# Second layer of a two-layer MLP: seven products in a row, then twelve sets, in place of four alternating blocks

## The chip, the cores and the metric

The kernel runs on one core of one Trainium2 chip. The metric is the time of one execution on the device in microseconds (us), the median of repeated runs. The core has TensorE (matrix products, PE in the profile, its weight loads PEld), VectorE (DVE), ScalarE (ACT), GpSimd (POOL) and SyncE (SP), which here issues every DMA.

## The reference

A linear attention, and two MLPs on its 4608 rows of 512 numbers:

```python
kv = np.einsum('bhsd,bhse->bhde', k_s, v)          # k_s, q_s: softmaxes of k and q
x = np.einsum('bhsd,bhde->bhse', q_s, kv)          # as 4608 rows of 512
h = np.maximum(x @ w_in1, 0.0);  x = (h * h) @ w_out1          # 512 -> 2048 -> 512
h = x @ w_in2;  out = (h * (1.0 / (1.0 + np.exp(-h)))) @ w_out2 # 512 -> 2048 -> 512
```

The weights come in as 64-bit floats. The change concerns the last line alone, the second layer.

## The kernel before, in words

Every operand of a large product is split into a high and a low part that TensorE takes (fp32r), and a product is three matmuls: high x high, high x low, low x high. `split` (L116) makes the parts: a cast on ScalarE (L117) gives the high one, a subtract on VectorE (L118) the low one.

The second layer takes 768 tokens at a time (`TS`), in six steps. In each step it goes through the 2048 hidden units in eight pairs of 128-blocks (`turns`, forward in one step and backward in the next). For a pair, `strassen` (L606) computes h = x @ w_in2 for two hidden blocks and two halves of 384 tokens with seven products in place of eight. Their names are A11, S1, S2, S4, S3, A12, A22, in the order in which they are run. A product (`product`, L597) is six matmuls of 128x384 at L602: two chunks of the inner dimension, three matmuls each. The weights wah and wal are kept per pair, two pairs at a time (`wa`, a `Cache`); in the first step they are made from w_in2, later they are loaded back. The operands x[0] to x[6] are made once per step from the first layer's result: `load_second` loads it (xr), `x_second` makes four differences (xt), and `X.split` splits all seven.

The products use two PSUM tiles, a and c, in turn: A11 on a, S1 on c, S2 on a, S4 on c, S3 on a, A12 on a fresh c, A22 on a. After each product ScalarE copies the tile to h, or VectorE adds it to h: copies at L613 (A11), L616 (S1), L620 (S2) and L636 (A22), adds at L623 (S4), L627 (S3) and L631 (A12). S2, S4, S3 and A22 accumulate onto what a or c holds, so the tile must have been copied before. `silu` (L870) makes g from a finished h: sigmoid (ScalarE, L872), multiply (VectorE, L873) and split into a g of high and low part. It runs twice per pair, for the first hidden block after A12 and for the second after A22.

The second product, y = g @ w_out2, is `y_mm` (L852). It is a generator of twelve sets per pair: for each of the two hidden blocks e and each of six groups of 128 tokens, `mm3` (L187 to L190) adds three matmuls of 128x512 to one of six PSUM banks Y. These hold the sums over all eight pairs; in the last pair of a step each bank is copied to a row tile o (L864, ScalarE and VectorE in turn), which SyncE writes out (L867). Together with a and c they fill all eight banks.

The sets of a pair are not run where they are created. `before` holds the generator of the previous pair, and `fill(n)` runs n sets of it. In `strassen`, `fill(sets)` stands after the second, the fourth and the sixth product and `fill(99)`, the rest, after the seventh; in the second layer `sets` is 3. `hook(n)` is called ahead of the product n and at the end (n = 7); in the second layer it loads, differences and splits the x of the next step at chosen pairs m. The order of the instructions on each engine is then made by a scheduler from the written order and the dependencies; it moves instructions ahead of others that must wait. Within an engine the order is fixed after that.

Of the kernel before, what the change touches and what calls it, by code (L numbers as in the profile page):

```python
# [10 lines left out]
F32 = mybir.dt.float32  # L11
F32R = mybir.dt.float32r
# [9 lines left out]
P = 128  # L22
TB = 512
# [8 lines left out]
def kernel(  # L32
# [15 lines left out]
    NT, DM = out.shape  # L48
# [10 lines left out]
    TS = 768  # L59
    TH = TS // 2  # L60
    assert SC == 4 and SM == TB and B * SL == TB and NB == B + 1 and SL <= P

    NP = NF // 2
# [5 lines left out]
    gpool = ctx.enter_context(tc.tile_pool(name="g", bufs=2))  # L69
# [11 lines left out]
    def take(shape, dt, name):  # L81

        at = idle.pop(0)
        t = spool.tile(shape, dt, tag=f"s{at}", name=name)
        slot_of[id(t)] = (at, t)
        return t
# [29 lines left out]
    def split(hi, lo, src):  # L116
        nc.scalar.copy(hi, src)  # L117
        nc.vector.tensor_sub(lo, src, f32(hi))  # L118
# [343 lines left out]
    def fill(n):  # L462
        for _ in range(n):
            next(before, None)
# [65 lines left out]
    wa = Cache(2, uses, make_wa, load_wa)  # L530
# [60 lines left out]
    def x_second(raw):  # L591
        t = [take([P, 2, NK // 2, TH], F32, "xt") for _ in range(2)]
        u = (slice(0, TH), slice(TH, TS))
        return X(TH, [raw[h][:, :, v] for v in u for h in range(2)],
                 [t[n // 2][:, n % 2] for n in range(4)], raw + t, 1)

    def product(ps, w, q, x, first):  # L597
        for c in range(2):
            k = slice(c * P, (c + 1) * P)
            wh, wl, xh, xl = w[0][:, q, k], w[1][:, q, k], x[:, 0, c], x[:, 1, c]  # L600
            for n, (l, r) in enumerate(((wh, xh), (wh, xl), (wl, xh))):
                nc.tensor.matmul(  # L602
                    ps, l, r, start=first and c == 0 and n == 0, stop=c == 1 and n == 2, skip_group_check=True
                )

    def strassen(w, x, th, h, g_of, hook, sets):  # L606

        new = lambda tag: ps_q.tile([P, TB], F32, tag=tag, name=tag)[:, 0:th]
        one, two = slice(0, th), slice(th, 2 * th)
        hook(0)  # L610
        a, c = new("a"), new("c")
        product(a, w, A11, x[0], True)
        nc.scalar.copy(h[:, 0, one], a)  # L613
        hook(1)
        product(c, w, S1, x[1], True)
        nc.scalar.copy(h[:, 1, two], c)  # L616
        fill(sets)
        hook(2)
        product(a, w, S2, x[2], False)
        nc.scalar.copy(h[:, 0, two], a)  # L620
        hook(3)
        product(c, w, S4, x[3], False)
        nc.vector.tensor_add(h[:, 0, two], c, h[:, 0, two])  # L623
        fill(sets)
        hook(4)
        product(a, w, S3, x[4], False)
        nc.vector.tensor_add(h[:, 1, two], a, h[:, 1, two])  # L627
        hook(5)
        c = new("c")
        product(c, w, A12, x[5], True)  # L630
        nc.vector.tensor_add(h[:, 0, one], c, h[:, 0, one])  # L631
        g = [g_of(h[:, 0])]
        fill(sets)
        hook(6)
        product(a, w, A22, x[6], False)
        nc.scalar.copy(h[:, 1, one], a)  # L636
        g.append(g_of(h[:, 1]))
        fill(99)
        hook(7)
        return g  # L640


    def relu2(h, src):
        nc.scalar.activation(h, src, AF.Relu)  # L644
        nc.scalar.activation(h, h, AF.Square)
        g = gpool.tile([P, 2, TB], F32R, tag="g", name="g")
        split(g[:, 0], g[:, 1], h)
        return g
# [143 lines left out]
    t = 0  # L792
    for j in range(1, NB):
        x, xs = xs, None
        for m, i in enumerate(turns[j - 1]):
            def hook(n):
                if (j, m, n) == (1, 0, 3):
                    wa.want(0)
                if n in (1, 6):
                    next(attend, None)  # L800
                    if j == 1 and (m, n) in ((1, 6), (3, 6)):
                        next(attend, None)
                if j < NB - 1:
                    if m == 4 and n == 0 and j == NB - 2:
                        XR[j + 1] = take([P, NK, TB], F32, "xr")
                        nc.sync.dma_start(out=XR[j + 1], in_=xld.rearrange("k p t -> p k t"))
                    if m == NP - 1:
                        if n == 0:
                            state["x"] = x_first(j + 1)
                            state["x"].split(2)  # L810
                        elif n == 4:
                            x.done(4)
                            state["x"].split(2)
                        elif n == 7:
                            x.done(NQ)
                            state["x"].split(3)
                else:
                    if m == 4 and n == 0:
                        state["raw"] = load_second(0)
                    elif m == 5 and n == 0:  # L820
                        state["x"] = x_second(state["raw"])
                        state["x"].split(2)
                    elif m == 6 and n == 0:
                        state["x"].split(1)
                    elif m == 7 and n == 0:
                        state["x"].split(1)
                    elif m == 7 and n == 4:
                        x.done(4)
                        state["x"].split(2)
                    elif m == 7 and n == 7:  # L830
                        x.done(NQ)
                        state["x"].split(1)

            state = {} if m == 0 else state
            h = hpool.tile([P, 2, TB], F32, tag="h", name="h")
            g = strassen(wa.tiles[0, i], x.x, TB // 2, h, lambda v: relu2(v, v), hook, 2)
            before = out_pair(j, m, i, g)
            t += 1
            wa.want(t)

            if j >= 2 and m < 6:
                next(ahead, None)
        xs = state["x"]
# [4 lines left out]
    lpool = ctx.enter_context(tc.tile_pool(name="l", bufs=2, reuse_waits="tile"))  # L848
# [3 lines left out]
    def y_mm(s, k, g, w):  # L852

        for e in range(2):
            first, last = k == 0 and e == 0, k == NP - 1 and e == 1
            for c in range(TS // P):
                if first:
                    pool, tag = (ps_o, f"o{c}") if c < NK else (ps_a, "pa")
                    Y[c] = pool.tile([P, DM], F32, tag=tag, name=f"y{c}")
                n = slice(c * P, (c + 1) * P)  # L860
                mm3(Y[c], g[e][:, 0, n], g[e][:, 1, n], w[:, 0, e], w[:, 1, e], first, last)
                if last:
                    o = lpool.tile([P, DM], F32, tag="y", name="o", bufs=4)
                    (nc.vector.tensor_copy if c % 2 else nc.scalar.copy)(o, Y[c])  # L864
                    at = s * TS + c * P
                    for r, rows in out_rows(order[at // TB], at % TB // P):
                        nc.sync.dma_start(out=rows, in_=o[r])  # L867
                yield

    def silu(h):  # L870
        z = lpool.tile([P, TS], F32, tag="z", name="z")
        nc.scalar.activation(z, h, AF.Sigmoid)  # L872
        nc.vector.tensor_mul(z, z, h)  # L873
        g = gpool.tile([P, 2, TS], F32R, tag="g", name="g")
        split(g[:, 0], g[:, 1], z)
        return g

    t1 = t
    for s in range(STEPS):
        x, state = xs, {}  # L880
        for m, i in enumerate(turns[NB - 1 + s]):
            def hook(n):
                if s + 1 == STEPS:
                    return
                if m == 1 and n == 0:
                    state["raw"] = load_second(s + 1)
                elif m == 4 and n == 0:
                    state["x"] = x_second(state["raw"])
                elif m == NP - 1 and n == 0:
                    state["x"].split(1)  # L890
                elif m == NP - 1 and n == 4:
                    x.done(4)
                    state["x"].split(3)
                elif m == NP - 1 and n == 7:
                    x.done(NQ)
                    state["x"].split(3)

            h = lpool.tile([P, 2, TS], F32, tag="h", name="h")
            g = strassen(wa.tiles[1, i], x.x, TH, h, silu, hook, 3)
            wb.want(t - t1)  # L900
            before = y_mm(s, m, g, wb.tiles[i,][0])
            t += 1
            wa.want(t)
        xs = state.get("x")
# [31 lines left out]
```

## Time and profile before

| | us |
|---|---|
| median of three runs | 1660.09 |
| the three runs | 1659.59, 1660.09, 1670.22 |
| the profiled execution | 1662.81 |
| its span on the core | 1661.0 |
| TensorE busy in the span | 1610.4 (97%) |
| VectorE, ScalarE busy | 996.2 (60%), 855.8 (52%) |
| TensorE's granted clock over the span | 0.999 |

A profile is one execution. Its timeline gives the start and the duration of each instruction, and in brackets how long the engine was idle before it and what released it. Matmuls are pipelined: the duration of one (0.33 to 0.40 us here) is longer than the distance to the next, so the distance between starts is what counts. The waits list, for a pair of instructions, who waited for whom: microseconds in total, how often, and the longest.

### The profile page before, as it was taken

Reading aid. Unit: us, or ns where it says so; the run is one execution under the profiler, and the core shown is the slowest. Engines: PE = TensorE matmul, PEld = TensorE weight load, DVE = VectorE, ACT = ScalarE, POOL = GpSimd, SP = SyncE. Lnnn points to the kernel's source line nnn. Section 1 sums busy time; section 2 is a strip of 40 time slices with the busy share of each in tenths; the row PEclk is TensorE's granted clock in tenths of the full one; section 3 lists DMA queues with packets and bytes.
Section 4 is the critical chain, followed back from the end, with each engine's and each line's share of the span. In section 5 each row is a group of like instructions: output and inputs, shape, how many; then the busy total and the mean of one; then the engine's idle time right before and its main releaser. Section 6 shows DMA issues by size and latency. Waiting matters only on the chain.

```text
span 1661.0 us, 24854 instructions
## 1 busy us (share of the span) xinstructions
PE 1610.4 (97%) x9624; PEld 1396.8 (84%) x9624; DVE 996.2 (60%) x1695; ACT 855.8 (52%) x1505; POOL 54.4 (3%) x150
## 2 busy tenths in 40 slices
PE   4999999999999999999999999999999999999999
PEld 3566888888888888889998889898988989999897
DVE  7999896886868687642436675345344344444333
ACT  4876675666666565654546554334334334334332
POOL 2000000000001000000000000000000000000000
PEclk9999999999999999999999999999999999999999
DMA  7776767678685776745346864543543543544621
GB/s 207 258 226 192 234 208 255 200 218 240 183 259 156 231 206 221 227 168 199 137 171 244 335 248 161 187 184 123 189 174 128 193 165 134 196 156 148 221 96 39
DMA packets 193510, 320.40 MB, mean 193 GB/s; under 512 B 113264, under 2 KB 142960, under 8 KB 188528
## 3 DMA queue, kind: packets, MB, share of 16 engines
q1 hardware_dynamic: 193392, 318.81, 57.6%
q8 instruction: 76, 1.25, 0.3%
q14 instruction: 42, 0.34, 0.1%
HBM read 248.51 MB, written 70.25 MB: 192 GB/s over the span
## 4 chain that ended last, share of the span: by engine, by line
PE 75%; DVE 10%; DMA 6%; ACT 5%; issue 2%; POOL 1%; SPq 0%; POOLq 0%; DVEq 0%; ACTq 0%
PE a L602 19%; PE c L602 14%; PE y L189 8%; PE y L190 8%; PE y L188 8%; PE op L189 5%; PE op L188 5%; PE op L190 5%; DMA raw<-in_moe_w_in_dram 3%; PE hp L655 2%; DMA raw<-in_moe_w_out_dram 2%; DVE g L118 1%; ACT raw L142 1%; DVE m L275 1%; DVE u L150 1%
## 5 line engine op out<-in xcount | busy, mean ns | idle before, releaser
L602 PE MATMUL a<-x,wah 128*128 128x256 f32 (+1 forms) x1792 | 397.7, 309 | 10.7 <-ACT h L636 6.4
L602 PEld LDWEIGHTS a<-x,wah 128*128 128x128 f32 x1792 | 313.4, 189 | 55.9 <-ACT h L636 11.7
L602 PE MATMUL c<-x,wah 128*128 128x256 f32 (+1 forms) x1344 | 293.4, 305 | 0.2 <-DVE h L623 0.2
L602 PE MATMUL a<-x,wal 128*128 128x256 f32 (+1 forms) x896 | 275.4, 307 | 0.0
L189 PE MATMUL op<-g,w 128*128 128x512 f32 x576 | 229.3, 398 | 3.1 <-DVE g L118 3.1
L188 PE MATMUL op<-g,w 128*128 128x512 f32 x576 | 229.2, 402 | 3.0 <-ACT g L117 3.0
L190 PE MATMUL y<-wb,g 128*128 128x512 f32 x576 | 227.8, 396 | 0.0
L189 PE MATMUL y<-wb,g 128*128 128x512 f32 x576 | 227.4, 395 | 0.0
L602 PEld LDWEIGHTS c<-x,wah 128*128 128x128 f32 x1344 | 225.0, 190 | 1.7 <-DVE h L623 0.6
L190 PE MATMUL op<-g,w 128*128 128x512 f32 x576 | 225.5, 391 | 0.0
L188 PE MATMUL y<-wb,g 128*128 128x512 f32 x576 | 223.2, 389 | 0.4 <-ACT wb L117 0.4
L602 PE MATMUL c<-x,wal 128*128 128x256 f32 (+1 forms) x672 | 204.8, 305 | 0.0
L872 ACT ACTIVATE z<-h 128x768 f32<-128x768 f32 x96 | 81.3, 847 | 226.9 <-DVE h L631 225.7
L602 PEld LDWEIGHTS a<-x,wal 128*128 128x128 f32 x896 | 168.9, 189 | 0.2
L623 DVE TENSOR_TENSOR h<-c,h 128x256 f32<-128x256 f32 (+1 forms) x112 | 53.7, 480 | 190.7 <-PE c L602 189.2
L644 ACT ACTIVATE h<-h 128x512 f32<-128x512 f32 x128 | 80.8, 632 | 105.1 <-DVE h L631 103.7
L118 DVE TENSOR_TENSOR g<-h,g 128x512 fp32r<-128x512 f32 x128 | 88.0, 688 | 77.7 <-ACT g L117 77.4
L118 DVE TENSOR_TENSOR g<-z,g 128x768 fp32r<-128x768 f32 x96 | 91.9, 957 | 67.3 <-ACT g L117 66.9
L627 DVE TENSOR_TENSOR h<-a,h 128x256 f32<-128x256 f32 (+1 forms) x112 | 53.5, 477 | 127.9 <-PE a L602 127.9
L620 ACT COPY h<-a 128x256 f32<-128x256 f32 (+1 forms) x112 | 47.1, 420 | 159.2 <-PE a L602 159.2
L190 PEld LDWEIGHTS op<-g,w 128*128 128x128 f32 x576 | 108.9, 189 | 23.7
L602 PEld LDWEIGHTS c<-x,wal 128*128 128x128 f32 x672 | 127.6, 190 | 0.0
(150 smaller groups left out, 2323.3 us busy)
## 6 DMA issues: line engine op xcount, KB each, us to landing
wah<-wad SPq DMA_DIRECT2D x72, 896.0 KB, 6.5
wal<-wad SPq DMA_DIRECT2D x72, 896.0 KB, 6.0
wb<-wbd SPq DMA_DIRECT2D x30, 1024.0 KB, 4.9
raw<-in_moe_w_in_dram SPq DMA_DIRECT2D x32, 512.0 KB, 5.3
raw<-in_moe_w_out_dram SPq DMA_DIRECT2D x32, 512.0 KB, 5.3
wad<-wah SPq DMA_DIRECT2D x16, 896.0 KB, 4.1
wad<-wal SPq DMA_DIRECT2D x16, 896.0 KB, 5.0
x1d<-o SPq DMA_DIRECT2D x18, 512.0 KB, 5.2
```

What stands on the lines that cost most here:

```text
L118: nc.vector.tensor_sub(lo, src, f32(hi))
L142: first = nc.scalar.activation(f32(lo32), lo32, AF.Copy, scale=2.0 ** -51, bias=2.0)
L188: nc.tensor.matmul(ps, lh, rh, start=first, stop=False)
L189: nc.tensor.matmul(ps, lh, rl, start=False, stop=False)
L190: nc.tensor.matmul(ps, ll, rh, start=False, stop=last)
L602: nc.tensor.matmul(ps, l, r, start=first and c == 0 and n == 0, stop=c == 1 and n == 2, skip_group_check=True)
L620: nc.scalar.copy(h[:, 0, two], a)
L623: nc.vector.tensor_add(h[:, 0, two], c, h[:, 0, two])
L627: nc.vector.tensor_add(h[:, 1, two], a, h[:, 1, two])
L644: nc.scalar.activation(h, src, AF.Relu)
L655: nc.tensor.matmul(hp, f32(w[:, s]), XR[0][:, c], start=c == 0, stop=c == NK - 1)
L872: nc.scalar.activation(z, h, AF.Sigmoid)
```

## The change

In the second layer the three numbers of sets that `strassen` runs between the products become (0, 0, 0): all seven products of a pair run in a row, and `fill(99)` then runs all twelve sets of the previous pair. The first layer keeps two sets in each place. Three things go with it. Every third g comes from a buffer of its own in `lpool`, so that three buffers take turns in place of two. The row tiles o have three buffers in place of four. And the hooks that prepare the next step's x are moved to later products: the differences from the start of the fifth pair to the last product of the fourth, the first split from the start of the last pair to the last product of the one before, and the next three from the fifth product of the last pair to its last. One empty line is added, so that the lines of `strassen` have numbers one higher.

```diff
         nc.scalar.copy(h[:, 1, two], c)
-        fill(sets)
+        fill(sets[0])
...
         nc.vector.tensor_add(h[:, 0, two], c, h[:, 0, two])
-        fill(sets)
+        fill(sets[1])
...
         g = [g_of(h[:, 0])]
-        fill(sets)
+        fill(sets[2])
...
-                    o = lpool.tile([P, DM], F32, tag="y", name="o", bufs=4)
+                    o = lpool.tile([P, DM], F32, tag="y", name="o", bufs=3)
...
-        g = gpool.tile([P, 2, TS], F32R, tag="g", name="g")
+        made.append(len(made) % 3)
+        g = (lpool.tile([P, 2, TS], F32R, tag="g", name="g", bufs=1) if made[-1] == 2 else
+             gpool.tile([P, 2, TS], F32R, tag="g", name="g"))
...
-    t1 = t
+    made, t1 = [], t
...
-                elif m == 4 and n == 0:
+                elif m == 3 and n == 6:
                     state["x"] = x_second(state["raw"])
-                elif m == NP - 1 and n == 0:
+                elif m == NP - 2 and n == 6:
                     state["x"].split(1)
-                elif m == NP - 1 and n == 4:
+                elif m == NP - 1 and n == 6:
                     x.done(4)
                     state["x"].split(3)
...
-            g = strassen(wa.tiles[1, i], x.x, TH, h, silu, hook, 3)
+            g = strassen(wa.tiles[1, i], x.x, TH, h, silu, hook, (0, 0, 0))
```

TensorE in the middle of a step, around the place between the second and the third product. Before, the end of a product on c, three sets (y, wb and g are the output bank, the weights w_out2 and the operand) and the next product on a:

```order
L602 MATMUL c<-x,wal 128x384
L188 MATMUL y_12553<-wb,g 128x512
L189 MATMUL y_12553<-wb,g 128x512
L190 MATMUL y_12553<-wb,g 128x512
L188 MATMUL y_12557<-wb,g 128x512
L189 MATMUL y_12557<-wb,g 128x512
L190 MATMUL y_12557<-wb,g 128x512
L188 MATMUL y_12561<-wb,g 128x512
L189 MATMUL y_12561<-wb,g 128x512
L190 MATMUL y_12561<-wb,g 128x512
L602 MATMUL a<-x,wah 128x384 x2
```

The same place in the changed kernel:

```order
L602 MATMUL c<-x,wal 128x384
L602 MATMUL c<-x,wah 128x384 x2
L602 MATMUL c<-x,wal 128x384
L602 MATMUL a<-x,wah 128x384 x2
L602 MATMUL a<-x,wal 128x384
```

The nine set matmuls are gone from between the products; all 36 of a pair stand behind its A22. In the first step the scheduler still puts some set matmuls between products, and in the last pair of the following steps it puts one between A12 and A22:

```order
L602 MATMUL c<-x,wah 128x384 x2
L602 MATMUL c<-x,wal 128x384
L188 MATMUL y_10763<-wb,g 128x512
L602 MATMUL a<-x,wah 128x384 x2
L602 MATMUL a<-x,wal 128x384
```

That last pair is also where the other two engines carry more than the evacuations of h. ScalarE in the changed kernel, from the copy of A11 (L614) to that of A22 (L637), with the casts for the next step's x between them:

```order
L614 COPY h<-a 128x384
L117 CAST x<-xt 128x768
L617 COPY h<-c 128x384
L117 CAST x<-xr 128x768
L621 COPY h<-a 128x384
L117 CAST x<-xt 128x768
L117 CAST x<-xr 128x768
L117 CAST x<-xt 128x768
L637 COPY h<-a 128x384
```

VectorE there, with the subtracts of the same splits between the adds of S4 (L624), S3 (L628) and A12 (L632):

```order
L118 TENSOR_TENSOR x<-xt,x 128x768 x2
L118 TENSOR_TENSOR x<-xr,x 128x768
L624 TENSOR_TENSOR h<-c,h 128x384
L118 TENSOR_TENSOR x<-xt,x 128x768
L628 TENSOR_TENSOR h<-a,h 128x384
L118 TENSOR_TENSOR x<-xr,x 128x768
L632 TENSOR_TENSOR h<-c,h 128x384
L118 TENSOR_TENSOR x<-xt,x 128x768
```

In both kernels these splits run within the last pair; before, sets stood between the products there, and now only the one set matmul does. In the other pairs of steps 2 to 6 the copies of A11, S1 and S2 follow each other directly on ScalarE, and so do the three adds on VectorE.

More of the change, by code (lines that the diff above doesn't have):

```diff
@@ L835 @@
             h = hpool.tile([P, 2, TB], F32, tag="h", name="h")
-            g = strassen(wa.tiles[0, i], x.x, TB // 2, h, lambda v: relu2(v, v), hook, 2)
+            g = strassen(wa.tiles[0, i], x.x, TB // 2, h, lambda v: relu2(v, v), hook, (2, 2, 2))
             before = out_pair(j, m, i, g)
```

## Prediction

> **What bounds the kernel now.** I read the page's first part, then the windows of the second layer, then the waits of TensorE, and last the timeline where products and sets of the second product follow each other.
>
> ```profile
> span 1661.0 us, 24854 instructions
> PE 1610.4 (97%) x9624; PEld 1396.8 (84%) x9624; DVE 996.2 (60%) x1695; ACT 855.8 (52%) x1505; POOL 54.4 (3%) x150
> ...
> 907.00:1032.00 125.00, 123.50 (x612) 110.43 (x613) 80.97 (x103) 61.88 (x86) 0.00 (x0) 1.00 0.71 261
> 1166.07:1291.72 125.65, 125.65 (x625) 113.08 (x625) 55.25 (x70) 46.85 (x74) 0.00 (x0) 1.00 0.45 163
> 1291.72:1417.37 125.65, 125.65 (x625) 113.08 (x625) 55.24 (x70) 46.86 (x74) 0.00 (x0) 1.00 0.46 164
> ```
> The second layer begins near 907 us and is six steps long. A middle step takes 125.65 us in which TensorE is busy all the time, at the full granted clock (1.00); VectorE works 55 of them and ScalarE 47. Only the first step has idle TensorE time, and the waits of its opening are all that there is:
>
> ```profile
> PE a L602 <- ACT h L620: 0.6, 1, 0.6
> PE y L188 <- ACT wb L117: 0.4, 1, 0.4
> PE a L602 <- DVE h L627: 0.4, 1, 0.4
> PE a L602 <- ACT h L613: 0.3, 1, 0.3
> ```
> So no wait can be removed that is worth more than 1.7 us. The change moves work on an engine that is already full; it can gain only if the same matmuls run closer together in another order. The timeline says that they do:
>
> ```profile
> 1291.56 0.51 PE L602 MATMUL a<-x,wah 128*128 128x384 f32 x2
> 1292.62 0.51 PE L602 MATMUL c<-x,wah 128*128 128x384 f32 x2
> 1293.66 0.39 PE L188 MATMUL y<-wb,g 128*128 128x512 f32 x1
> 1295.74 0.51 PE L602 MATMUL a<-x,wah 128*128 128x384 f32 x2
> ...
> 915.05 0.51 PE L602 MATMUL c<-x,wah 128*128 128x384 f32 x2
> 916.09 0.51 PE L602 MATMUL a<-x,wah 128*128 128x384 f32 x2
> ...
> 1650.44 0.39 PE L190 MATMUL y<-wb,g 128*128 128x512 f32 x1
> 1655.20 0.39 PE L190 MATMUL y<-wb,g 128*128 128x512 f32 x1
> ```
> The first column is the start. Interleaved, a product of six matmuls right after sets takes 1292.62 - 1291.56 = 1.06 us, the product behind it 1.04, and nine matmuls of three sets 2.08 (231 ns each). In a long row of products, in the opening of the layer, six take 1.04 (173.3 ns each); in the long row of sets at the very end, the 21 between 1650.44 and 1655.20 take 4.76 (226.7 each). Matmuls seem to be spaced wider for a while after each change from 384 to 512 columns and back.
>
> **The price of a switch.** A step has 8 pairs of 42 product matmuls and 36 set matmuls. At the row speeds that is 336 x 0.1733 + 288 x 0.2267 = 123.5 us; the step takes 125.65. The 2.1 us left are spread over 32 returns (four blocks of products and four of sets in each pair): 0.066 us for one return, there and back.
>
> A rule of the Trainium skill speaks against this: "TensorE: Matmul & The Clock Gate", section "Back-to-back issue gap", gives the gap of warm matmuls as columns / 2.4 + 2.5 ns, whatever came before; by it a return would cost nothing, and my estimate from it is a step of 117 us. The trace has 173 and 227 ns where this page gives 163 and 216, and a step of 125.65.
>
> **The change part by part.** *Rows.* In steps 2 to 6 each pair keeps one return instead of four. 5 x 24 = 120 returns go. In the order of the changed kernel one set matmul stands between the last two products of the last pair of a step, which puts 4 back: 116 x 0.066 = 7.7 us. In the first step the order still splits several rows; of some 24 returns there about 12 go: 0.8 us. Removed: 8.5 us. The bounds are nothing, if the wide spacing has another cause than the switch, and 8 x 6 x 3 x 0.066 = 9.5.
>
> *Evacuations in the row.* The products alternate between the PSUM tiles a and c. Before, the sets stood between two uses of a tile; now product k + 2 waits for the evacuation of product k with only one product, 1.04 us, as cover. Five such waits come in each pair: three on ScalarE copies, one of which also feeds a VectorE add, and two on the adds. What they need shows in the opening, where the kernel before already runs three products in a row:
>
> ```profile
> 914.88 0.33 PE L602 MATMUL a<-x,wal 128*128 128x384 f32 x1
> 915.25 0.56 DVE L627 TENSOR_TENSOR h<-a,h 128x384 f32<-128x384 f32 x1 [0.81 <-PE a L602]
> 915.92 0.36 PEld L602 LDWEIGHTS a<-x,wah 128*128 128x128 f32 x2
> ...
> 912.99 0.34 PE L602 MATMUL a<-x,wal 128*128 128x384 f32 x1
> 913.37 0.48 ACT L620 COPY h<-a 128x384 f32<-128x384 f32 x1 [0.64 <-PE a L602]
> 913.89 0.30 PEld L602 LDWEIGHTS a<-x,wah 128*128 128x128 f32 x2 [0.89 <-ACT h L620]
> 913.90 0.62 PE L602 MATMUL a<-x,wah 128*128 128x384 f32 x2 [0.57 <-ACT h L620]
> ```
> The add starts 0.37 after its product's last matmul starts and ends 0.93 after it, at 915.81. The first weight load of the product that waits for such an add, one product later, begins at 915.92 and its matmul at 916.09, in an unbroken row: the add was in time by about 0.1 us. The copy is done 0.86 after (913.37 + 0.48 - 912.99), earlier still by 0.08. The last two rows show the failure: two products on a with none between, the load starts 0.04 after the copy, and TensorE idles 0.57. So an evacuation on a free engine costs nothing, with 0.1 us to spare for an add. That holds if ScalarE and VectorE are free, so I ask what else they do during the 7.3 us of products. The rows of their work:
>
> ```profile
> L872 ACT ACTIVATE z<-h 128x768 f32<-128x768 f32 x96 | 81.3, 847 | 226.9 <-DVE h L631 225.7
> L873 DVE TENSOR_TENSOR z<-z,h 128x768 f32<-128x768 f32 x96 | 91.8, 957 | 46.8 <-ACT z L872 46.7
> L117 ACT CAST g<-z 128x768 fp32r<-128x768 f32 x96 | 80.3, 836 | 75.5 <-DVE z L873 65.6 <-PE a L602 6.0 <-PE y L190 3.7
> L118 DVE TENSOR_TENSOR g<-z,g 128x768 fp32r<-128x768 f32 x96 | 91.9, 957 | 67.3 <-ACT g L117 66.9
> ```
> The chain of one g (sigmoid, multiply, cast, subtract) is 3.6 us. Both start at the end of the products and run beside 12 sets, 36 x 0.227 = 8.2 us. The second g needs the buffer that the first six sets read (4.1 us), so its cast starts about 4.5 us into the sets, and its subtract ends at about 6.5. Both engines are free again 1.7 us before the next products: the third g buffer is what makes this possible, and no cost stands on the path. Ordinary pairs: 0.
>
> *Last pair of a step.* Here the splits of the next x (a cast of 0.84 and a subtract of 0.96 each) stand between the evacuations. I walk it in their order from the start of the pair. ScalarE: copy to 1.7, cast, copy at 2.4, cast, copy of S2 done at 4.0 where the product S3 on a wants it at 4.0; VectorE: the subtract of the fourth x ends at 4.6, the add of S4 follows to 5.1 (A12 wants c at 5.1), another subtract, and the add of S3 ends at 6.4, when A22 wants a at 6.3 (one set matmul is put there). I take 0.1 us for each of 5 such pairs: 0.5; the bounds are 0 and one whole split, 0.96, in each: 4.8.
>
> *First step.* Weights are still being made there (casts of 1.7 us, subtracts of 2.0). The opening must still wait for the first wb, and the copies of the second pair now stand behind the casts of g. I take 0.3 us lost on balance; the bounds are a gain of the 1.7 us of waits above and a loss of 4, two long subtracts.
>
> *Output rows, three buffers.* In the middle of the kernel six rows of a step go out in 24 transfers that SyncE issues one after the other:
>
> ```profile
> out_dram<-o SPq DMA_DIRECT2D x108, 64.0 KB, 1.7
> ...
> 1158.69 11.65 SPq L867 DMA_DIRECT2D out_dram<-o  x24
> ...
> 1654.20 4.23 SPq L867 DMA_DIRECT2D out_dram<-o  x6
> 1655.62 0.69 DVE L864 COPY o<-y 128x512 f32<-128x512 f32 x1 [0.67 <-PE y L190]
> 1656.48 0.59 ACT L864 COPY o<-y 128x512 f32<-128x512 f32 x1 [0.95 <-DMA out_dram<-o]
> 1657.38 0.69 DVE L864 COPY o<-y 128x512 f32<-128x512 f32 x1 [1.06 <-DMA out_dram<-o]
> ```
> The issue of one row of y takes 11.65 / 6 = 1.94 us and its landing 1.7, so with three buffers the fourth to sixth copies wait longer. The fourth waits until about 2 us before the first add of the next pair; the fifth stands behind all three copies of that pair, the sixth behind its adds, and the banks are wanted again only in the next row of sets, 1 us after the sixth. Behind them in SyncE's queue are loads for two pairs later. Cost 0; without that 1 us it would be the wait of one bank, some 1 us in each of 5 steps. At the end nothing covers it: the fifth and sixth copy already wait for the first and second transfer (1656.48, 1657.38). With three buffers the fourth starts at 1656.48, the fifth at 1657.38, the sixth at about 1658.2, 0.8 later. Cost 0.8.
>
> **Sum.** -8.5 + 0.5 + 0.3 + 0.8 = -6.9 us. The profiled execution took 1662.8 us (span 1661.0), 2.7 over the median of the three runs, 1660.1. I expect 1655.9 for a profiled execution like that and **1653.2 us** for the median. That is 0.4% less. A measurement of this kernel can tell about 1% from no change, 16.6 us, and the removable part is smaller than that by any bound.
>
> **Rivals.**
> *The spacing doesn't follow the switches.* If the wide spacing comes with the position in the layer, or returns in the middle of long rows, the row gains nothing and the small losses stay: 1660.1 + 1.6 = 1661.7. For it: each long row that I have stands in the opening or at the end. Against: the pattern in the middle is the same at every block, and the opening has both other engines busy. By the Trainium skill's rule of the gap ("TensorE: Matmul & The Clock Gate", same section) the order would not matter either, so it stands with this rival.
>
> *The evacuations are late in ordinary pairs (slower).* The place is the wait of product k + 2 on a VectorE add; the price is what the waits of the opening took, 0.3 us for one (the wait for L613); and it decides once an add is later than its spare 0.1 us, as it would be behind any other instruction. One such wait in each of 47 pairs: 47 x 0.3 = 14.1, and the time is 1653.2 + 14.1 = 1667.3. It passes the gain from 6.9 / 47 = 0.15 us a pair. For it: five tight waits a pair, 235 in all, and a copy feeding an add. Against: the row at 915 us is unbroken. Two a pair would be over 1% slower, 1681.
>
> *The edges cost more.* The last pairs lose a whole split (4.8) and the first step 4 us: 1653.2 + 4.3 + 3.7 = 1661.2. For it: those are the pairs in which the engines carry other work; against: before, that work cost nothing.
>
> **How the numbers follow.** Forecast 0.70; no effect of the spacing 0.10; late evacuations 0.12; costlier edges 0.08. The forecast's own bounds are 1649.7 (all 9.5 of the returns and the 1.7 of the waits go, the tail's 0.8 stays) and 1657.2 (half of what the edges can cost). Two rivals end near 1661.5 and are taken in; the slower one is left out. Range 1649.5 to 1662. Faster by over 1% needs more than all bounds together: 0.02. Slower by over 1% is the slower rival with two waits a pair: 0.05. Within 1%: 0.93.
>
> **What would show it.** Right: a middle step of about 124.2 us with TensorE busy throughout, six products after the first at 1.04 us, and sets at 226.7 ns from about the tenth matmul on; TensorE's waits in steps 2 to 6 only at the last pair, around 0.1 us; the last copies of y waiting for transfers. Wrong: a repeated wait of a or c for an add or a copy of h in ordinary pairs, or spacing of 231 ns inside the long rows.

## The result, and the profile after

| | before | after |
|---|---|---|
| median | 1662.92 us (9 runs, 1655.51 to 1670.22) | 1654.71 us (9 runs, 1652.67 to 1657.16) |
| after / before | | 0.995, 95% interval 0.9935 to 0.9965 |
| profiled execution | 1662.81 us | 1654.71 us |

The changed kernel is 0.5% faster. The interval excludes no change, so these runs tell half a percent, where the prediction took 1% for the least that could be told; the size is within the 1% to which the prediction gave a chance of 0.93. The first part of the page of the changed kernel:

```profile
span 1652.9 us, 24906 instructions
PE 1601.9 (97%) x9624; PEld 1392.4 (84%) x9624; DVE 993.1 (60%) x1695; ACT 856.5 (52%) x1505; POOL 51.5 (3%) x150
```

The same 9624 matmuls keep TensorE busy for 8.5 us less, and the span is 8.1 us shorter. Where the 8.1 us went shows when both kernels are cut at the same places: at the first product of the second layer, at the first product of its second step, at the last matmul and at the end. The windows of the kernel before (the columns are length, then busy time and count of each engine, granted clock, DMA share, GB/s):

```profile
894.72:1020.36 125.64, 123.96 (x614) 110.34 (x612) 85.52 (x108) 66.37 (x93) 0.00 (x0) 1.00 0.76 278
1020.36:1656.56 636.20, 636.20 (x3157) 572.01 (x3155) 270.28 (x344) 231.68 (x368) 0.00 (x0) 1.00 0.43 154
1656.56:1661.03 4.47, 0.38 (x2) 0.00 (x0) 0.69 (x1) 0.51 (x1) 0.00 (x0) 1.00 0.62 231
```

The same of the changed kernel, and below them one middle step:

```profile
893.55:1018.71 125.16, 123.18 (x613) 109.99 (x612) 86.74 (x110) 67.33 (x94) 0.00 (x0) 1.00 0.78 286
1018.71:1647.76 629.05, 629.05 (x3157) 569.39 (x3155) 264.81 (x340) 232.27 (x365) 0.00 (x0) 1.00 0.44 154
1647.76:1652.90 5.14, 0.39 (x2) 0.00 (x0) 1.38 (x2) 0.59 (x1) 0.00 (x0) 0.90 0.54 202
1267.15:1391.41 124.26, 124.26 (x625) 112.58 (x624) 54.72 (x70) 47.26 (x74) 0.00 (x0) 1.00 0.46 163
```

The start of the layer comes 1.17 us earlier (893.55 against 894.72). Nothing ahead of it was changed, and in the other kernels of this study that leave the first layer alone it lies between 893.39 and 897.94, so 1.17 us is within the spread and is not counted for the change. The first step is 0.48 us shorter, steps 2 to 6 are 7.15 shorter with TensorE busy all the time in both, and the tail is 0.67 longer. A middle step (the second to the fifth) takes 124.21 to 124.26 us in place of 125.65.

The timeline shows how the step became shorter with nothing idle in it. The first set of a row, the tenth set matmul after it, the last, and then the start of each product of the next row:

```profile
1290.00 0.39 PE L188 MATMUL y<-wb,g 128*128 128x512 f32 x1
1292.08 0.39 PE L188 MATMUL y<-wb,g 128*128 128x512 f32 x1
1297.98 0.39 PE L190 MATMUL y<-wb,g 128*128 128x512 f32 x1
1298.20 0.51 PE L602 MATMUL a<-x,wah 128*128 128x384 f32 x2
1299.27 0.51 PE L602 MATMUL c<-x,wah 128*128 128x384 f32 x2
...
1303.43 0.51 PE L602 MATMUL c<-x,wah 128*128 128x384 f32 x2
1304.50 0.51 PE L602 MATMUL a<-x,wah 128*128 128x384 f32 x2
1305.54 0.39 PE L188 MATMUL y<-wb,g 128*128 128x512 f32 x1
```

The first nine set matmuls take 2.08 us (231 ns each), the other 27 take 6.12 (226.7 each). The first product takes 1.07, the four from 1299.27 to 1303.43 take 1.04 each, A12 1.07 (1303.43 to 1304.50; this one has another cause, told under "Why the prediction was right") and A22 1.04. The wide spacing is still there, but once per pair instead of four times.

The waits of TensorE in the whole second layer, in microseconds in total, times and the longest:

```profile
PE a L602 <- ACT h L614: 1.0, 2, 0.8
PE c L602 <- DVE h L624: 0.5, 1, 0.5
PE y L188 <- ACT wb L117: 0.5, 1, 0.5
```

All four waits lie in the first step, between 901 and 975 us.

### The profile page after: what moved, and what is told of

The parts are those of the page before. It is cut to its first block, busy times and chain, and to the rows that moved or that the text cites. A ratio compares the mean times of both kernels' runs of the same rounds, so it can differ in the third digit from the quotient of the medians.

```text
span 1652.9 us, 24906 instructions
## 1 busy us (share of the span) xinstructions
PE 1601.9 (97%) x9624; PEld 1392.4 (84%) x9624; DVE 993.1 (60%) x1695; ACT 856.5 (52%) x1505; POOL 51.5 (3%) x150
## 4 chain that ended last, share of the span: by engine, by line
PE 60%; DVE 6%; DMA 3%; ACT 3%; issue 1%; POOL 0%; SPq 0%; DVEq 0%; POOLq 0%; ACTq 0%
PE a L602 16%; PE c L602 12%; PE y L190 8%; PE y L189 8%; PE y L188 8%; PE op L189 3%; PE op L188 3%; PE op L190 3%; DMA raw<-in_moe_w_in_dram 1%; DMA raw<-in_moe_w_out_dram 1%; DMA c<-wf 1%; DVE g L118 1%; ACT h L645 1%; DVE x L118 1%; ACT h L646 0%
## 5 line engine op out<-in xcount | busy, mean ns | idle before, releaser
L624 DVE TENSOR_TENSOR h<-c,h 128x256 f32<-128x256 f32 (+1 forms) x112 | 53.6, 479 | 253.1 <-PE c L602 251.6
L190 PEld LDWEIGHTS op<-g,w 128*128 128x128 f32 x576 | 108.4, 188 | 23.4
L190 PEld LDWEIGHTS y<-wb,g 128*128 128x128 f32 x576 | 108.1, 188 | 22.4
L188 PEld LDWEIGHTS y<-wb,g 128*128 128x128 f32 x576 | 108.1, 188 | 22.0 <-ACT wb L117 0.8
L189 PEld LDWEIGHTS op<-g,w 128*128 128x128 f32 x576 | 109.1, 189 | 20.3 <-DVE g L118 7.0
```

Of the source, the lines that this page charges most:

```text
L188: nc.tensor.matmul(ps, lh, rh, start=first, stop=False)
L189: nc.tensor.matmul(ps, lh, rl, start=False, stop=False)
L190: nc.tensor.matmul(ps, ll, rh, start=False, stop=last)
```

## The experiments

Theory: matmuls are spaced wider for a while after each change between 384 and 512 columns, and the kernel gains what the removed changes cost. Rivals: something else in the change brings the gain (buffers, hooks); or the wide spacing belongs to a change of operands, banks or position; or evacuations of a and c come late and eat it. Below, a return is one block of products and one of sets, counted in the order of TensorE's instructions.

**Undo the rows alone.** All else of the change stays:

```diff
-            g = strassen(wa.tiles[1, i], x.x, TH, h, silu, hook, (0, 0, 0))
+            g = strassen(wa.tiles[1, i], x.x, TH, h, silu, hook, (3, 3, 3))
```

> The changed kernel with three sets again after the second, fourth and sixth product; the third g buffer, three row tiles and the moved hooks stay. Theory (each return from products to sets and back costs 0.066 us): 33 returns in a middle step again in place of 9, a middle step of 125.7 us, about 1662 us in all. Rival (the buffers or the moved hooks brought the gain): the step stays at 124.2 us.

Time of one execution: 1662.78 us, span 1661.0. A middle step:

```profile
1145.26:1270.91 125.65, 125.65 (x625) 113.07 (x624) 55.30 (x71) 47.06 (x75) 0.00 (x0) 1.00 0.46 163
```

It is the step of the kernel before to the hundredth. The gain sits in the order of the sets; buffers and hooks bring none of it without the rows.

**The rows alone,** in the kernel before (its `strassen` takes one number), with two buffers of g, four row tiles and the hooks where they were:

```diff
-            g = strassen(wa.tiles[1, i], x.x, TH, h, silu, hook, 3)
+            g = strassen(wa.tiles[1, i], x.x, TH, h, silu, hook, 0)
```

> The kernel before with the rows alone: two g buffers, four row tiles, the old places of the hooks. Theory (the third g buffer hides a wait that has cover anyway): the second g of a pair waits for all twelve sets and is cast in the first 1 us of the next products, while the first copy is wanted only after 1.3 us; a middle step of 124.3 us with 10 returns, and a tail that is 0.7 us shorter than in the changed kernel: 0.5 us faster than it. Rival (the third buffer is needed): the cast and the subtract of the late g delay the copies of the next pair, 0.3 us in each of 47 pairs, and the step is 126.6 us.

1657.27 us median (11 runs, 1653.43 to 1661.59) against 1664.01 of the kernel before on the same chip: ratio 0.9956, interval 0.9941 to 0.9971. Its first step and a middle one:

```profile
893.53:1020.02 126.49, 123.80 (x613) 109.86 (x612) 85.88 (x109) 66.37 (x93) 0.00 (x0) 1.00 0.78 283
1144.53:1269.00 124.47, 124.47 (x626) 112.65 (x625) 55.13 (x70) 47.94 (x74) 0.00 (x0) 1.00 0.47 165
```

The middle step is 124.47 to 124.51, with TensorE busy throughout (124.47 in 124.47). With two buffers the second g of a pair waits for all twelve sets. Its cast on ScalarE falls into the next row of products, whose first matmul starts at 1175.58, and is done 0.24 us before the copy of A11 starts:

```profile
1175.78 0.83 ACT L117 CAST g<-z 128x768 fp32r<-128x768 f32 x1 [3.24 <-PE y L190]
...
1176.85 0.48 ACT L613 COPY h<-a 128x384 f32<-128x384 f32 x1 [0.23 <-PE a L602]
```

So in ordinary pairs two buffers of g are enough, for the reason that the expectation gave. It also had this kernel 0.5 us faster than the changed one, and that was missed: in the two traces the tail is 0.7 us shorter, but steps 2 to 6 are 1.1 longer and the opening 1.3. The middle step is some 0.25 us longer, all of it in the last pair. There is one return more (ten against nine), and there the copy of A11 stands behind the cast of the late g and one of a split of x at its old place, so that S2 loses 0.2 us. What came with the rows is worth that much in a step; no comparison of times here resolves it.

**Two blocks in place of one,** (0, 6, 0): six sets after S4, six after A22:

```diff
-            g = strassen(wa.tiles[1, i], x.x, TH, h, silu, hook, (0, 0, 0))
+            g = strassen(wa.tiles[1, i], x.x, TH, h, silu, hook, (0, 6, 0))
```

> Changed kernel with six sets after the fourth product (S4) and six after the seventh, instead of twelve after the seventh: 16 or 17 returns in a middle step, all between long blocks (18 set matmuls, 18 or 24 product matmuls). Price per return (0.066 us) theory: middle step 123.5 + 17 x 0.066 = 124.6 us, no waits of TensorE in ordinary pairs. If the price per return grew with the number of sets in the block instead of being paid once, the step would stay at 124.2; if the loss came from positions and not from returns, the same. A single look resolves this in the middle step (steps repeat within about 0.05 us), not in the total, where +2 us (1656.7) is within the scatter.

Time of one execution: 1657.63 us. A middle step:

```profile
1164.00:1288.62 124.62, 124.62 (x626) 112.62 (x626) 54.64 (x70) 47.12 (x75) 0.00 (x0) 1.00 0.47 165
```

Steps of 124.61 to 124.63 with no wait, as the price per return said. From 17 returns to 32 the step grows by 1.04 us, 0.069 for each.

**Seven blocks,** two sets after each of the first six products. `strassen` gets six numbers, and the first layer's are written so that it keeps its places:

```diff
+        fill(sets[0])
         hook(1)
         product(c, w, S1, x[1], True)
         nc.scalar.copy(h[:, 1, two], c)
-        fill(sets[0])
+        fill(sets[1])
...
-            g = strassen(wa.tiles[0, i], x.x, TB // 2, h, lambda v: relu2(v, v), hook, (2, 2, 2))
+            g = strassen(wa.tiles[0, i], x.x, TB // 2, h, lambda v: relu2(v, v), hook, (0, 2, 0, 2, 0, 2))
...
-            g = strassen(wa.tiles[1, i], x.x, TH, h, silu, hook, (0, 0, 0))
+            g = strassen(wa.tiles[1, i], x.x, TH, h, silu, hook, (2, 2, 2, 2, 2, 2))
```

> The other way: two sets after each of the first six products, some 46 returns in a middle step. Theory: 123.5 + 46 x 0.066 = 126.5 us a step, somewhat less (126.1) if the wide spacing has not run out after six matmuls; about 1665 us in all. Rival (the spacing follows the position in the layer or the load of the other engines, not the switches): between 124.2 and 125.7 us.

Time of one execution: 1674.13 us; the middle step is slower than both numbers:

```profile
1166.81:1294.25 127.44, 127.00 (x625) 111.90 (x624) 55.17 (x71) 46.45 (x75) 0.00 (x0) 1.00 0.45 161
```

With 46 returns the step lies 3.9 us over the 123.5 of the row speeds, in two parts. The spacing of all matmuls of the step, summed by block, gives 1.8 us: a block of six set matmuls costs 29 ns, not 41, and a product of six after it 7 ns, not 26; short blocks cost less per return. (In a block of nine, too, the first six set matmuls lie 29 ns over: a short block ends before the wide spacing has run out.) The other 2.1 us are waits. 1.1 of them are at three places of the step, where a set matmul waits for the cast of g (0.79 together) and the one behind it comes 0.11 late. The other 1.0 recurs in seven of the eight pairs; the timeline there, with TensorE's weight loads (PEld):

```profile
1307.73 0.33 PE L602 MATMUL a<-x,wal 128*128 128x384 f32 x1
...
1308.11 0.48 ACT L640 COPY h<-a 128x384 f32<-128x384 f32 x1 [0.94 <-PE a L602]
...
1308.43 0.34 PE L602 MATMUL c<-x,wah 128*128 128x384 f32 x1
...
1308.64 0.30 PEld L602 LDWEIGHTS a<-x,wah 128*128 128x128 f32 x2 [0.19 <-ACT h L640]
1308.64 0.44 PE L602 MATMUL a<-x,wah 128*128 128x384 f32 x1
```

The scheduler put only four matmuls of c between A22 and the next matmul on a, so the load of weights for a waits until the copy of A22 is done (1308.59). The matmul comes 210 ns after the one before, 37 late, and the one behind it 281 ns after it in place of 173: 0.14 us for a matmul that was 0.04 late. This order was to raise the number of returns alone, and it did not. Without the waits the step would be at 125.3 us, inside the rival's band and below the kernel before with its 32 returns, so its time decides nothing between the two theories; the expectation allowed for shorter wide stretches, but only down to 126.1. For the theory speaks the spacing itself: the six set matmuls behind a change are 229, 233, 236, 224, 231 and 236 ns apart here, and the first six of a block of nine in the kernel before are the same to the nanosecond.

**One width for both kinds.** The set matmuls are cut to the 384 columns of a product; the last 128 of the 512 output columns are neither computed nor written. Once with rows (0, 0, 0), once with (3, 3, 3):

```diff
-                mm3(Y[c], g[e][:, 0, n], g[e][:, 1, n], w[:, 0, e], w[:, 1, e], first, last)
+                mm3(Y[c][:, 0:TH], g[e][:, 0, n], g[e][:, 1, n], w[:, 0, e, 0:TH], w[:, 1, e, 0:TH], first, last)
```

> Changed kernel with the set matmuls 384 columns wide instead of 512 (the last 128 of the 512 output columns are neither computed nor written). Then products and sets have one width. Width theory: the matmuls of both kinds are spaced 173.3 ns from the first on, a middle step takes 624 x 0.1733 = 108.1 us. Rival, the price belongs to the change of operands or of PSUM banks: 108.1 + 9 x 0.066 = 108.7.

> As the kernel before it (sets 384 columns wide, the last 128 output columns left out), with three sets after the second, fourth and sixth product again: 33 returns in a middle step. Width theory: still 108.1 us a middle step, equal to the kernel with rows to within 0.1. Rival, the price belongs to the change of operands or banks: 108.1 + 33 x 0.066 = 110.3, 1.6 us more than with rows.

Times of one execution each: 1564.74 us with rows, 1565.94 interleaved. A middle step with rows (9 returns):

```profile
1246.43:1354.95 108.52, 108.52 (x626) 108.25 (x625) 54.26 (x70) 46.92 (x75) 0.00 (x0) 1.00 0.53 187
```

The same step interleaved (33 returns):

```profile
1243.07:1351.59 108.52, 108.52 (x626) 108.14 (x626) 54.85 (x71) 46.61 (x75) 0.00 (x0) 1.00 0.52 186
```

Equal, as in steps 3 to 5 altogether (108.47 to 108.55 and 108.46 to 108.51), where the rival wanted 1.6 us between them. In step 2 the one with rows is 0.3 us longer (108.79 against 108.46), and over steps 2 to 6 it is 0.7 longer, against the rival's direction. Of the 1.2 us between the two times 0.8 arise before the second layer. The timeline of the interleaved one, at a change from sets on y to a product on a and back:

```profile
1151.85 0.33 PE L188 MATMUL y<-wb,g 128*128 128x384 f32 x1
...
1153.41 0.51 PE L602 MATMUL a<-x,wah 128*128 128x384 f32 x2
...
1154.45 0.51 PE L602 MATMUL c<-x,wah 128*128 128x384 f32 x2
...
1155.49 0.33 PE L188 MATMUL y<-wb,g 128*128 128x384 f32 x1
```

Nine set matmuls take 1.56 us and each product 1.04, from the first matmul on: 173.3 ns throughout. Operands, lines and banks change here as before, and nothing is lost. The price belongs to the change of the column count. (Both steps are 0.4 over the expected 108.1: with rows 0.3 of it are small delays inside the product rows, interleaved 0.2 are one wait for the copy of A22.)

**Four row tiles again,** the rest as changed:

```diff
-                    o = lpool.tile([P, DM], F32, tag="y", name="o", bufs=3)
+                    o = lpool.tile([P, DM], F32, tag="y", name="o", bufs=4)
```

> The changed kernel with four row tiles again. Theory (the last copies of y wait for transfers because there are three): the stretch from the last matmul to the end is 4.5 us in place of 5.1, the middle step unchanged at 124.2 us, 0.7 us faster than the changed kernel, which single runs cannot tell. Rival (the end is set by the last transfer alone): 5.1 us as with three.

1655.99 us median (6 runs, 1654.34 to 1658.85), ratio to the kernel before 0.9955, interval 0.9938 to 0.9972. The end of the changed kernel, from its last matmul:

```profile
1647.76 0.39 PE L190 MATMUL y<-wb,g 128*128 128x512 f32 x1
1647.80 0.69 DVE L865 COPY o<-y 128x512 f32<-128x512 f32 x1 [1.65 <-DMA out_dram<-o]
1648.59 0.59 ACT L865 COPY o<-y 128x512 f32<-128x512 f32 x1 [1.86 <-DVE o L865]
1649.22 0.69 DVE L865 COPY o<-y 128x512 f32<-128x512 f32 x1 [0.73 <-ACT o L865]
```

With four row tiles, the last matmul and the last copy, and then the window of this tail:

```profile
1650.11 0.39 PE L190 MATMUL y<-wb,g 128*128 128x512 f32 x1
1650.94 0.69 DVE L865 COPY o<-y 128x512 f32<-128x512 f32 x1 [1.07 <-DMA out_dram<-o]
```

```profile
1650.11:1654.59 4.48, 0.39 (x2) 0.00 (x0) 0.69 (x1) 0.51 (x1) 0.00 (x0) 1.00 0.62 231
```

With three tiles the fourth of the last six copies already waits for a transfer, and the last starts 1.46 us after the last matmul; with four, 0.83 after. The tail is 4.48 against 5.14, as in the kernel before. Middle steps are the same (124.23 to 124.31). The theory holds: four tiles save 0.66 us at the end by the trace. The times do not show it: against the kernel before the ratio is 0.9955, with three tiles 0.995, and in the profiled execution the first layer ended 1.35 us later and the first step took 0.8 longer. No run shows a version whose time beats the changed kernel's.

**Rows in the first layer too,** where a product is six matmuls of 256 columns:

```diff
-            g = strassen(wa.tiles[0, i], x.x, TB // 2, h, lambda v: relu2(v, v), hook, (2, 2, 2))
+            g = strassen(wa.tiles[0, i], x.x, TB // 2, h, lambda v: relu2(v, v), hook, (0, 0, 0))
```

> Changed kernel with no sets between the products of the first layer either, where products are 256 columns wide and take about 0.73 us each. The cover of an evacuation is one product: 0.73 us here against 1.04 in the second layer, while copy and add (0.37 us until the engine starts, then about 0.37 to 0.42 of work, some 0.05 until the weight load) need about 0.8 to 0.85. Theory that cover decides: waits of a and c for copies and adds of h of about 0.1 us, four to five in each of the first layer's 64 pairs: 25 to 32 us, less the returns saved (at most 9): slower by 15 to 25 us, about 1675. Rival, evacuations have slack enough at any width: faster by the returns, about 1648 to 1651.

Time of one execution: 1670.56 us, 15.9 more than the changed kernel. From the first product of the first layer to the first of the second it takes 764.70 us against 750.11. TensorE's waits in that stretch, those of products for evacuations:

```profile
PE c L602 <- ACT h L617: 6.5, 10, 1.1
PE a L602 <- ACT h L614: 4.6, 9, 2.3
PE c L602 <- DVE h L624: 3.7, 7, 0.9
...
PE a L602 <- ACT h L621: 0.8, 1, 0.8
PE a L602 <- DVE h L628: 0.5, 3, 0.2
```

Products now wait for the copies of S1 and A11 and the adds of S4, 16.1 us in all; in the changed kernel they wait 6.3 us there, half of it for copies of A22. The list leaves out the short ones: the distances between starts hold some 70 more places (123 against 50) where two product matmuls are about 223 ns apart in place of 120, spread over the layer. Summed over all product matmuls of the layer, the distances lie 21.9 us over 120 ns a matmul, against 5.3 in the changed kernel: 16.6 us more, of which the returns saved give some back. The time is that of the theory (15 to 25 us), its make-up only in part: fewer and longer waits than four of 0.1 in every pair. One of the longer waits, for a copy of S1 that stands behind the making of the next x on ScalarE:

```profile
323.99 0.64 ACT L419 COPY xr<-xp 128x288 f32<-128x288 f32 x2
...
324.62 0.64 ACT L117 CAST x<-xt 128x512 fp32r<-128x512 f32 x1
325.14 0.39 ACT L617 COPY h<-c 128x256 f32<-128x256 f32 x1
...
325.58 0.50 PE L602 MATMUL c<-x,wah 128*128 128x256 f32 x2 [1.10 <-ACT h L617]
```

So the rival of late evacuations is real; it decides where the cover is 0.72 us (six matmuls at 120 ns) and the engines have other work, and does not where it is 1.04 and they have little. Which of the two differences counts for more, no run here separates.

## Why the prediction was right

| step of the prediction | predicted | measured |
|---|---|---|
| steps 2 to 6: returns (-7.7) and last pairs (+0.5) | -7.2 | -7.15 |
| first step: returns (-0.8) and late weights (+0.3) | -0.5 | -0.48 |
| tail with three row tiles | +0.8 | +0.67 |
| sum | -6.9 | -6.96 |
| middle step | 124.2 | 124.21 to 124.26 |

1653.2 us was predicted and 1654.71 measured, inside the range. The base differs more than the step: the kernel before now has a median of 1662.92, 2.8 over the three runs that the forecast started from, and the medians are 8.2 us apart where 6.9 was forecast. The stages of the trace carry the sum of 6.96. That it meets 6.9 so closely is partly luck: the term of the rows is right by its mechanism, but the +0.5 of the last pairs and the -0.5 of the first step are not, as told below.

*The price of a switch* was right and its cause is shown. In a middle step of the kernel before, summed over all matmuls, each of 32 set blocks lies 41 ns over 226.7 a matmul and each of 32 product blocks 26 ns over 173.3: 0.067 us a return. The changed kernel pays the same 41 and 26 at its long blocks, eight times a step, and less than the 41 at the single set matmul. Matmul by matmul the spacing behind a change is the same in both kernels: within a few ns at each of the nine set matmuls and each of the six of a product. The steps with 17 and 32 returns lie where this price puts them (123.5 + 17 x 0.067 = 124.6, 123.5 + 32 x 0.067 = 125.6), the one with 9 is 0.1 over it (next point), and with equal widths the price is gone. So the first rival, spacing that doesn't follow the switches, is refuted. The Trainium skill ("TensorE: Matmul & The Clock Gate", section "Back-to-back issue gap") gives columns / 2.4 + 2.5 ns as the gap of an isolated matmul, which the prediction left unsaid, and about 131 ns for 512 columns in a stream of weight loads and matmuls; neither figure has a part for what came before. The runs agree that order has no part where the width stays (173.3 ns in both 384-column kernels) and show one where it changes; the steady 226.7 ns at 512 columns lies above both figures. The price of 0.067 us holds for blocks of at least nine set matmuls; in blocks of six it is 29 and 7 ns.

*Evacuations in ordinary pairs* were put at 0 with 0.1 us to spare for an add. At one of the adds that spare was not there. The changed kernel in an ordinary pair:

```profile
1302.22 0.33 PE L602 MATMUL c<-x,wal 128*128 128x384 f32 x1
...
1302.66 0.56 DVE L624 TENSOR_TENSOR h<-c,h 128x384 f32<-128x384 f32 x1 [6.50 <-PE c L602]
...
1303.26 0.34 PE L602 MATMUL a<-x,wal 128*128 128x384 f32 x1
1303.27 0.35 PEld L602 LDWEIGHTS c<-x,wah 128*128 128x128 f32 x2
1303.43 0.51 PE L602 MATMUL c<-x,wah 128*128 128x384 f32 x2
1303.63 0.56 DVE L628 TENSOR_TENSOR h<-a,h 128x384 f32<-128x384 f32 x1 [0.42 <-PE a L602]
```

The add of S4 starts 0.44 after its product's last matmul, not 0.37 as that of S3 (1303.63 against 1303.26), and is done at 1303.22; the load that waits for it starts 0.05 later, and its matmul still on time at 1303.43. So at this add nothing was left to spare. The prediction took 0.37 from the add of S3; the kernel before has the 0.44 for the add of S4 too (1293.49 to 1293.93), where sets gave it cover. A12 behind it is the product of 1.07 us. Averaged over the 36 unbroken rows of steps 2 to 6, the first product of a row lies 26 ns over the row speed, A12 14, and the other five 2 together. With sets between S4 and A12 (blocks of 18 and 24) only the first 26 are there; in the kernel with rows and one width, where a change costs nothing, A12 lies 26 over. So the loss goes with A12 in a row, the one product that waits for this add: some 16 ns a pair, 0.1 us a step. As a sum that is little; it was on the brink of the 0.14 us that a really late copy cost in the seven-block kernel.

*Last pair of a step:* 0.1 us each was put there; the step has about that loss (in the one shown, 0.74 us over 123.5 less 9 x 0.067 = 0.14), but nearly all of it is in the ordinary pairs as just shown. In the last pair only the short blocks around the one set matmul are a little over. A right sum from a wrong place. *First step:* -0.5 was met, but that is luck: kernels with these rows have 123.99 (rows in the first layer too), 125.16, 125.97 (four row tiles) and 126.49 us there (rows alone, old hooks and buffers), so its size is not established by one execution. The count was low as well: the first step has 29 returns before and 15 after, so 14 go and not 12. *Output rows:* 0 in the middle is right (three or four tiles, same steps), the tail is as worked out.

*The third g buffer* was called what makes the free engines possible, and with it both are indeed free before the next products. But the gain does not need it: with two buffers the second g is cast in the first 1.1 us of the next row, before ScalarE's first copy is due, and that costs nothing except in the last pair, where a split follows it (0.2 us a step).

The rival of late evacuations had 0.12; in the second layer it did not come, in the first layer the rows make the stretch 14.6 us longer. Costlier edges did not come either.

## What to carry to other kernels

When an engine is busy all the time, look at the distance between the starts of its instructions, not at its waits: a stage can still hold time in how the instructions are ordered, and the total of the removable distance bounds the gain before anything is built (here 2.1 us a step, 1.4 of it won). Grouping matmuls of one width also takes cover away: it paid here where the product between two uses of a tile was longer than the evacuation with its latency (1.04 us against 1.00 for the latest add), and did not where a product was 0.72 us long. Weigh a sub-percent change by stages of the trace cut at the same instruction, since the total carries a microsecond or more of scatter from stages that nobody touched. Read the latency of each evacuation by itself: one of the five here was 0.07 us later than the one that the prediction measured.

## What was not expected of the hardware

- After a change from 384 to 512 columns the first nine matmuls are 224 to 236 ns apart and then 226.7; after the change back the first six are 171 to 185 and then 173.3. A block of six set matmuls pays 29 ns of the 41. With 384 columns on both sides neither occurs. What in TensorE causes it, no run here tells.
- A matmul that waited for an evacuation costs more than its lateness: the one behind it comes 281 ns after it in place of 173 (384 columns), 223 in place of 120 (256 columns), about 0.1 us each time.
- VectorE's add started 0.37 us after the last matmul of S3 and 0.44 after that of S4 in the same row, with the engine free in both cases, and 0.38 and 0.44 in the kernel before. No run here tells why.
